# Short runs of zero matmuls in nine tile shapes at the head of TensorE's list, and other orders of the score matmuls of three chunks

## The chip, the cores and the metric

The kernel runs on one core of a Trainium2 chip. The metric is the device time of one execution in microseconds (us). The kernel before took 857.0 us, the median of two runs (855.85 and 858.14 us). The trace below is one further execution under the hardware profiler; its span is 857.2 us.

## What is computed

Two layers, each an attention block and an MLP block with residuals, over 2048 tokens of width 576, in bf16. Attention has 32 heads of 18 elements and a sliding window of 256 keys; the MLP has 4608 hidden units and tanh GELU.

```python
B, S, D, H, W, F = 1, 2048, 576, 32, 256, 4608      # Dh = 18
def A(x, wqkv, wo):                                  # attention
    q, k, v = (x @ wqkv) split in 3 and in heads
    scores = einsum("bhqd,bhkd->bhqk", q, k) * Dh ** -0.5
    mask = (i - j >= 0) & (i - j < W)
    return merge(softmax(where(mask, scores, -1e9)) @ v) @ wo
def Bm(x, w1, b1, w2, b2):                           # MLP
    return gelu(layernorm(x) @ w1 + b1) @ w2 + b2
for layer in range(2):
    x = x + A(layernorm(x), A_wqkv, A_wo)
    x = x + Bm(layernorm(x), B_w1, B_b1, B_w2, B_b2)
```

## The kernel before

The tokens are cut into chunks of 512 (four tiles of 128), four chunks for each layer, numbered k = 0 to 7 through both layers. For each chunk `qkv` makes q, k and v, `E` (`E0` for chunk 0) runs scores, exponentials, masks and the product with v for eight groups of four heads, `tail` applies `wo` and the residual, and `G_part` and `mm2` run the MLP in three parts. The stages of neighbouring chunks are interleaved.

Each engine runs its list strictly in order. The lists are made by a planner, `Plan.schedule`, from estimated costs, priorities and a table of nudges; `Sched.add` puts semaphore waits where one engine needs another's result. TensorE's work carries a mode: `f` is the full array of 128 rows and 128 columns, `r` four row tiles (32x128 each), `c` four column tiles (128x32 or 128x20), `h` two row tiles (64x128). A run of matmuls in one mode that fills all its tiles at once is called a wave below: four matmuls in `r` and `c`, two in `h`, one in `f`.

At the head TensorE has nothing to compute until the first tokens have been loaded and normalised. As soon as the tile `warm` has been set to zero (L657) it runs zero matmuls: `zero` (L662, two of 256 columns for each of the four PSUM banks 7, 6, 5 and 4), then `warm_fn` (L671, 256 columns each), whose number `keep_warm` works out from the planner's own estimates. Then come the transposes of the normalised tokens (L732), and the q, k and v matmuls of chunk 0 (L794), which wait for the loads of `wqkv`. The PSUM banks are handed out by the planner in the same way.

`scores` (L923) makes one unit of scores: for each of four heads j, which lie in the row tiles 32j to 32j+31, it multiplies the keys of one tile by the queries of one to three tiles. A unit has one or two parts n, with another key tile each. Head j has a PSUM bank of its own, and the two parts lie beside each other in it. One semaphore increment stands on the unit's last matmul; ScalarE's exponential (L933) waits for it, then GpSimd masks the diagonal blocks (L954), then the product with v follows (L975). In the chunks 1, 2 and 3 each group has three units: two with parts of 384 and 128 columns, one with 256 and 256. That is 16 and 8 units for each chunk.

Of the kernel before, what the change touches and what calls it, by code (L numbers as in the profile page):

```python
# [40 lines left out]
class Sched:  # L41
# [23 lines left out]
    def add(self, eng, fn, reads=(), writes=(), dma=None, ring=4, own=False):  # L65
        waits = {}

        def want(ev):
            c, v, _e = ev
            if waits.get(c, 0) < v:  # L70
                waits[c] = v

        for r in reads:
            lw = self.last_write.get(r)
            if lw is not None and not (eng == "pe" and lw[2] == "pe"):
                want(lw)
        for w in writes:
            for rd in self.readers.get(w, ()):
                if own or rd[2] != eng or rd[3]:
                    want(rd[:3])  # L80
            lw = self.last_write.get(w)
            if lw is not None and (own or not (eng == "pe" and lw[2] == "pe")):
                want(lw)
        if dma is None:
            assert eng != "sp"
            c = self.cnt[eng]
            amount = 1
        else:
            rg = self.ring(eng, dma, ring)
            c = rg.sems[rg.i % rg.k]  # L90
            rg.i += 1
            amount = 16
            if c.val > 0:
                want((c, c.val, None))
        wl = []
        wd = self.waited[eng]
        for cc, v in waits.items():
            if wd.get(cc, 0) >= v:
                continue
            wd[cc] = v  # L100
            wl.append((cc, v))
        c.val += amount
        by = None if dma is not None else eng
        ev = (c, c.val, by)
        self.steps[eng].append(Step(eng, fn, wl, c, amount))
        for w in writes:
            self.last_write[w] = ev
            self.readers[w] = []
        for r in reads:
            self.readers.setdefault(r, []).append((c, c.val, by, dma is not None))  # L110
        return ev
# [324 lines left out]
def build_kernel(nc, A_x, A_wqkv, A_wo, B_x, B_w1, B_b1, B_w2, B_b2, out):  # L436
# [38 lines left out]
    add = PL.add  # L475
# [66 lines left out]
    def sb(name, shape, dtype):  # L542
        return nc.alloc_sbuf_tensor(name, shape, dtype)
# [24 lines left out]
    warm = sb("warm", [P, P], BF16)  # L568
# [7 lines left out]
    def bank(i):  # L576
        if isinstance(i, Bank):
            i = i.no
        return ps[:, i * 512:(i + 1) * 512]

    FILL = (7, 6, 5, 4)
    OUT = (7, 6, 5, 4)
# [3 lines left out]
    def two(b):  # L586
        return ps[:, b.no * 512:(b.no + 2) * 512].rearrange("p (j c) -> p j c", j=2)
# [18 lines left out]
    def q_of(k):  # L606
        return (qx, "qx") if k == 1 else (qT, "q")

    def k_of(A):

        if Q1 <= A < Q1 + 2:
            return kx[:, A - Q1, :, :], f"kx{A - Q1}"
        sl = A if A < Q1 else (A - 2) % KS
        return kT[:, :, sl, :], f"k{sl}"
# [35 lines left out]
    for i in range(NQN):  # L650
        add("pool", lambda e, i=i: e.memset(qn[:, i, :].rearrange("p (h e) -> p h e", e=32)[:, :, DH:32], 0.0),
            writes=[f"qn{i}h{h}" for h in range(2)], cost=0.5, prio=-9)
    for b in range(2):
        add("dve", lambda e, b=b: e.memset(wqkv[64 * b:64 * b + 64, 4, :].rearrange("p (w s d) -> p w s d", w=3, s=2)[:, :, 1 - b, :], 0.0),
            writes=[f"w{w}C{b}" for w in "qkv"], cost=0.5, prio=-8)
# [3 lines left out]
    def zero(e, b):  # L659
        ins = None  # L660
        for c in range(2):
            ins = e.matmul(bank(b)[:, c * 256:(c + 1) * 256], warm[:, :], warm[:, :].unsqueeze(1).to_broadcast([P, 2, P]), start=True, stop=True)  # L662
        return ins
    for i in OUT:
        b = Bank((i,))
        add("pe", lambda e, b=b: zero(e, b), reads=["warm"], writes=[b], cost=0.42, lat=0.2, prio=-7, alloc=[b])

    def warm_fn(e, bk, n):
        ins = None
        for _ in range(n):  # L670
            ins = e.matmul(bank(bk)[:, 0:256], warm[:, :], warm[:, :].unsqueeze(1).to_broadcast([P, 2, P]), start=True, stop=True)  # L671
        return ins
# [238 lines left out]
    def scores(k, g, parts, prio, gs=None):  # L911
        l, t0, nt = CH[k]
        T0 = l * NT + t0
        qs, qname = q_of(k)
        sl = slots.popleft()
        bs = [Bank(SC, True), Bank(SC, True)]

        def fn(e):
            ins = None
            for n, (so, qo, nq, col) in enumerate(parts):  # L920
                gg = gs[n] if gs else g
                for j in range(4):
                    ins = e.matmul(two(bs[j // 2])[:, j % 2, col:col + nq * 128], k_of(T0 + so)[0][32 * j:32 * j + 32, gg, :],  # L923
                                   qs[32 * j:32 * j + 32, gg, qo * 128:(qo + nq) * 128], start=True, stop=True, tile_position=(32 * j, 0),
                                   skip_group_check=True)
            return ins
        rd = [f"{qname}{qo + i}" for (so, qo, nq, col) in parts for i in range(nq)] + [k_of(T0 + p[0])[1] for p in parts]
        ncol = sum(p[2] for p in parts) * 128
        add("pe", fn, reads=rd, writes=bs, cost=0.01 + ncol * 0.00042, prio=prio, lat=0.15, alloc=bs, fifo="pa", mode="r", after=[f"p{sl}h{h}" for h in range(2)] + [f"p{sl}m{m}" for m in range(3)])
        lo = min(p[3] for p in parts)  # L930
        hi = max(p[3] + p[2] * 128 for p in parts)
        for h2 in range(2):
            add("act", lambda e, h2=h2: e.activation(pT[:, sl, 2 * h2:2 * h2 + 2, lo:hi], two(bs[h2])[:, :, lo:hi],  # L933
                                                     ACT.Exp, scale=SCALE),
                reads=[bs[h2]], writes=[f"p{sl}h{h2}"], cost=0.07 + 2 * (hi - lo) * 0.00083, lat=0.17,
                fifo="act", prio=prio)
        blk = {}
        for (so, qo, nq, col) in parts:
            for q in range(nq):
                if qo + q == so:  # L940
                    blk[col + q * 128] = "d"
                elif qo + q == so + 2:
                    blk[col + q * 128] = "o"
        runs = []
        for c in sorted(blk):
            if runs and runs[-1][0] == blk[c] and runs[-1][1] + runs[-1][2] * 128 == c:
                runs[-1][2] += 1
            else:
                runs.append([blk[c], c, 1])
        for mi, (kind, col, nb) in enumerate(runs):  # L950
            sgn = 1 if kind == "d" else -1
            pat = [[0, 4]] + ([[0, nb]] if nb > 1 else []) + [[sgn, 128]]
            ap = pT[:, sl, :, col:col + nb * 128]
            add("pool", lambda e, ap=ap, pat=pat, sgn=sgn, kind=kind: e.affine_select(  # L954
                ap, ap, pattern=pat, compare_op=(ALU.is_ge if kind == "d" else ALU.is_gt), fill=0.0, base=0, channel_multiplier=-sgn),
                reads=[f"p{sl}h0", f"p{sl}h1"], writes=[f"p{sl}m{mi}"], cost=0.12 + 0.475 * nb, prio=prio)
        return sl
# [244 lines left out]
    for i in range(n0):  # L1202
# [5 lines left out]
        cost=0.5, prio=-1)  # L1208
    dma("sp", b2bc[:, :], bass.AP(tensor=B_b2.tensor, offset=B_b2.offset, ap=[[0, P], [1, D]]), reads=["k3"], writes=["b2"], cls="b", ring=2,
        cost=0.5, prio=-1)  # L1210
    add("pe", lambda e: e.transpose(bank(bb).bitcast(BF16)[:, 0:NF], b1in, ident[0:NF, 0:NF]), reads=["b1i", "ident"], writes=[bb],
        cost=0.1, lat=0.22, prio=5, alloc=[bb])
# [104 lines left out]
def bass_interleave_layers__sliding_block__mixer_channel_mlp__prompt_kernel(  # L1317
    nc,
    A_x,
    A_wqkv,  # L1320
    A_wo,
    B_x,
    B_w1,
    B_b1,
    B_w2,
    B_b2,
    out,
):
    build_kernel(nc, A_x, A_wqkv, A_wo, B_x, B_w1, B_b1, B_w2, B_b2, out)
# [28 lines left out]
```

## Time and profile before

| | |
|---|---|
| runs | 855.85 and 858.14 us, median 857.0 |
| the profiled execution | span 857.2 us |
| DVE, ACT, POOL busy | 46%, 70%, 44% |
| DMA | mean 140 GB/s |

The page gives each engine's busy time, the chain of work that ended last, and the costliest groups. The timeline gives, in order of time, the start and the length of a group of equal instructions on one engine, and in brackets how long the engine had been idle before it and what it waited for. The durations of single matmuls overlap: a matmul of 288 columns shows some 0.286 us, though the next one of the same kind starts 0.12 us later. So prices are taken from start to start, or from the length of a long group divided by its count. "x20" counts instructions, four of which make one wave in the modes `r` and `c`.

### The profile page before, as it was taken

Reading aid. Unit: us, or ns where it says so; the run is one execution under the profiler, and the core shown is the slowest. Engines: PE = TensorE matmul, PEld = TensorE weight load, DVE = VectorE, ACT = ScalarE, POOL = GpSimd, SP = SyncE. Lnnn points to the kernel's source line nnn. Section 1 sums busy time; section 2 is a strip of 40 time slices with the busy share of each in tenths; the row PEclk is TensorE's granted clock in tenths of the full one; section 3 lists DMA queues with packets and bytes.
Section 4 is the critical chain, followed back from the end, with each engine's and each line's share of the span. In section 5 each row is a group of like instructions: output and inputs, shape, how many; then the busy total and the mean of one; then the engine's idle time right before and its main releaser. Section 6 shows DMA issues by size and latency. Waiting matters only on the chain.

```text
span 857.2 us, 28212 instructions
## 1 busy us (share of the span) xinstructions
PE 842.7 (98%) x12180; PEld 517.6 (60%) x12180; DVE 398.6 (46%) x949; ACT 599.1 (70%) x745; POOL 379.1 (44%) x569
## 2 busy tenths in 40 slices
PE   8999999999999999999999999999999999999998
PEld 6555556556566565666665655656556556556556
DVE  6777434655257352672445723564226534162013
ACT  4988887778757787476773877748885689853730
POOL 4776554375235662263421654426534276322100
PEclk9999999999999999999999999999999999999999
DMA  7899435461596534967258443595345963346320
GB/s 198 195 184 149 127 124 145 115 165 45 166 182 124 154 94 121 186 133 191 85 124 195 89 149 122 104 223 130 112 157 116 225 187 109 119 133 186 116 84 29
DMA packets 181996, 119.86 MB, mean 140 GB/s; under 512 B 107504, under 2 KB 181872, under 8 KB 181872
## 3 DMA queue, kind: packets, MB, share of 16 engines
q1 hardware_dynamic: 181872, 118.05, 55.1%
q8 instruction: 96, 1.57, 0.8%
q14 instruction: 28, 0.23, 0.1%
HBM read 90.10 MB, written 2.36 MB: 108 GB/s over the span
## 4 chain that ended last, share of the span: by engine, by line
PE 91%; DMA 3%; DVE 2%; ACT 2%; POOL 1%; issue 1%; SPq 0%; DVEq 0%; POOLq 0%; ACTq 0%
PE ps L1115 31%; PE ps L775 25%; PE ps L778 11%; PE ps L835 8%; PE ps L923 6%; PE ps L975 5%; PE ps L1070 4%; DMA xnTm<-xn 2%; ACT pT L933 1%; DMA wqkv<-in_A_wqkv_dram 1%; PE ps L794 1%; DVE x_res L1047 1%; POOL pT L954 1%; DMA x_res<-qn 1%; DVE st_all L684 1%
## 5 line engine op out<-in xcount | busy, mean ns | idle before, releaser
L954 POOL TENSOR_SCALAR_AFFINE_SELECT pT<-pT 128x1024 bf16<-128x1024 bf16 (+1 forms) x370 | 282.8, 786 | 219.3 <-ACT pT L933 217.1
L933 ACT ACTIVATE pT<-ps 128x1024 bf16<-128x1024 f32 (+1 forms) x372 | 344.9, 999 | 42.4 <-PE ps L923 41.7
L1115 PE MATMUL ps<-xnTm,w_sb 64*128 64x512 bf16 x2592 | 291.8, 376 | 0.6 <-DVE x_res L1050 0.3
L1125 ACT ACTIVATE hT<-ps,b1col 128x512 bf16<-128x512 f32 x276 | 168.0, 688 | 176.5 <-PE ps L1115 176.4
L1115 PEld LDWEIGHTS ps<-xnTm,w_sb 64*128 64x128 bf16 x2592 | 127.5, 94 | 140.7 <-issue 4.0
L775 PE MATMUL ps<-w_sb,hT 128*128 128x288 bf16 x1410 | 188.5, 287 | 0.9 <-DVE vA L847 0.8
L1047 DVE TENSOR_TENSOR x_res<-ps,x_res 128x288 f32<-128x288 f32 x224 | 100.5, 454 | 180.7 <-PE ps L775 122.3
L775 PEld LDWEIGHTS ps<-w_sb,hT 128*128 128x128 bf16 x1410 | 130.5, 98 | 50.5 <-issue 16.9
L778 PE MATMUL ps<-w_sb,hT 128*32 128x288 bf16 x2808 | 96.5, 286 | 0.2
L835 PE MATMUL ps<-wqkv,xnTa 64*128 64x288 bf16 x1296 | 91.3, 283 | 2.2 <-DVE vA L847 0.9
L859 DVE CAST qn<-ps 128x288 bf16<-128x288 f32 x112 | 46.4, 451 | 86.4 <-PE ps L835 78.5
L986 DVE STREAM_TRANSPOSE oq<-ps 128x512 f32<-128x512 f32 x64 | 45.8, 716 | 84.6 <-PE ps L975 83.9
L778 PEld LDWEIGHTS ps<-w_sb,hT 128*32 128x32 bf16 x2808 | 72.5, 97 | 14.9 <-issue 3.4
L835 PEld LDWEIGHTS ps<-wqkv,xnTa 64*128 64x128 bf16 x1296 | 61.4, 94 | 30.0 <-issue 3.9
L923 PE MATMUL ps<-qT,kT 32*128 32x128 bf16 (+2 forms) x1248 | 63.2, 274 | 2.5 <-ACT pT L933 2.5
L697 POOL TENSOR_SCALAR vtmp<-mv_all 128x1 f32<-128x1 f32 (+2 forms) x45 | 9.2, 204 | 120.5 <-DVE mv_all L688 119.1
L1131 POOL TENSOR_TENSOR x_res<-x_res,b2bc 128x576 f32<-128x576 f32 x32 | 40.2, 1276 | 37.6 <-ACT hT L1125 37.4
L684 DVE BATCH_NORM_STATS2 st_all<-x_res 128x6 f32<-128x288 f32 (+1 forms) x128 | 53.5, 446 | 3.0 <-DMA x_res<-in_A_x_dram 2.1
L847 DVE CAST vA<-ps 128x288 bf16<-128x288 f32 x60 | 25.3, 448 | 55.1 <-PE ps L835 49.1
L975 PE MATMUL ps<-pT,vA 128*20 128x384 bf16 (+2 forms) x1440 | 50.4, 275 | 0.3 <-DVE vA L847 0.2
L923 PEld LDWEIGHTS ps<-qT,kT 32*128 32x128 bf16 x1248 | 19.2, 92 | 41.4 <-issue 26.9
L1070 PE MATMUL ps<-wo_sb,attT 64*128 64x288 bf16 x576 | 42.5, 283 | 0.3
(58 smaller groups left out, 478.4 us busy)
## 6 DMA issues: line engine op xcount, KB each, us to landing
w_sb<-in_B_w_dram SPq DMA_DIRECT2D x46, 864.0 KB, 6.1
w_sb<-in_B_w_dram SPq DMA_DIRECT2D x48, 768.0 KB, 4.8
w_sb<-in_B_w_dram SPq DMA_DIRECT2D x96, 48.0 KB, 4.6
wqkv<-in_A_wqkv_dram SPq DMA_DIRECT2D x3, 576.0 KB, 5.6
x_res<-in_A_x_dram SPq DMA_DIRECT2D x3, 576.0 KB, 4.3
wqkv<-in_B_w_dram SPq DMA_DIRECT2D x2, 864.0 KB, 5.2
out_dram<-x_res SPq DMA_DIRECT2D x12, 144.0 KB, 1.9
xnTm<-xn SPq DMA_TRANSPOSE x36, 2.8
```

The lines of the kernel that those rows point to most:

```text
L684: add("dve", lambda e, i=i, s=s: e.bn_stats(st_all[:, t, i, :], s[:, t, i * HB:(i + 1) * HB]), reads=res, writes=[f"st{t}_{i}"], cost=0.37 ...
L775: return e.matmul(bank(b)[:, 0:HB], lhs, rhs, start=start, stop=stop, skip_group_check=True)
L778: ins = e.matmul(bank(b)[32 * j:32 * j + 32, 0:HB], lhs[:, 32 * j:32 * j + 32], rhs, start=start, stop=stop, tile_position=(0, 32 * j), sk ...
L835: ins = e.matmul(bank(bs[o])[:, 0:HB], xnTa[r:r + 64, c, i * 128:(i + 1) * 128], wqkv[r:r + 64, c, col:col + HB], start=(c == 4), stop=(ph ...
L923: ins = e.matmul(two(bs[j // 2])[:, j % 2, col:col + nq * 128], k_of(T0 + so)[0][32 * j:32 * j + 32, gg, :], qs[32 * j:32 * j + 32, gg, qo ...
L933: add("act", lambda e, h2=h2: e.activation(pT[:, sl, 2 * h2:2 * h2 + 2, lo:hi], two(bs[h2])[:, :, lo:hi], ACT.Exp, scale=SCALE), reads=[bs ...
L954: add("pool", lambda e, ap=ap, pat=pat, sgn=sgn, kind=kind: e.affine_select(ap, ap, pattern=pat, compare_op=(ALU.is_ge if kind == "d" else ...
L975: ins = e.matmul(bank(bo)[32 * j:32 * j + VW, qo * 128:(qo + nq) * 128], vA[:, (T0 + so) % VS, 8 * j + g, :], pT[:, sl, j, col:col + nq * ...
L1047: add("dve", lambda e: e.tensor_tensor(x_res[:, t, sl], bank(b)[:, 0:HB], x_old[:, t, sl], ALU.add), reads=[b] + ([f"xin{t}"] if first els ...
L1070: ins = e.matmul(bank(bs[o])[:, 0:HB], attT[r:r + 64, c, i * 128:(i + 1) * 128], wo_sb[r:r + 64, c, col:col + HB], start=(ph == 0 and c == ...
L1115: ins = e.matmul(bank(bks[i])[:, 0:n], w1_sb[r:r + 64, sls[i], col:col + 128], xnTm[r:r + 64, k % 2, c, 0:n], start=(c == 4), stop=(ph == ...
L1125: add("act", lambda e, ff=ff, hd=hd, bk=bk: e.activation(hd[:, 0:n], bank(bk)[:, 0:n], ACT.Gelu_apprx_tanh, bias=b1col[:, ff:ff + 1]), rea ...
```

## The change

Twenty probe steps are put at the head of TensorE's list, ahead of `zero`. Each step runs a number of waves in one tile shape, on the zero tile `warm`, into the four banks that `zero` uses afterwards; nothing reads them. There are nine shapes: r (32x128), c (128x32), h (64x128), f (128x128), u (128x64), s (32x64), m (64x64), q (32x32) and t (64x32). The steps have 397 matmuls in all, each with its own load of weights, of 64 to 512 columns, and the shape changes between most of them. To the planner a step costs 0.01 us.

The score matmuls of three chunks are issued in another order; the same matmuls run. In chunk 1 the two parts alternate from head to head, and then the other halves follow. In chunk 2 the second part runs through the heads backwards. In chunk 3 the second part runs ahead of the first. All other chunks keep their order.

```diff
+    SIZES = {"r": (32, 128), "c": (128, 32), "h": (64, 128), "f": (128, 128), "u": (128, 64), "s": (32, 64), "m": (64, 64), "q": (32, 32), "t": (64, 32)}
+
+    def step(e, bks, md, n):
+        ins = None
+        rs, cs = SIZES[md]
+        for r in range(0, 128, rs):
+            for c in range(0, 128, cs):
+                rhs = warm[r:r + rs, 0:n] if n <= 128 else warm[r:r + rs, 0:n // 4].unsqueeze(1).to_broadcast([rs, 4, n // 4])
+                ins = e.matmul(bank(bks[r // rs])[c:c + cs, 0:n], warm[r:r + rs, c:c + cs], rhs, start=True, stop=True,
+                               tile_position=(r, c), skip_group_check=True)
+        return ins
+
+    PROBE = (("r", 288, 6), ("r", 64, 8), ("c", 64, 8), ("f", 64, 8), ("r", 512, 3), ("s", 288, 4), ("r", 288, 3), ("q", 288, 4), ("r", 288, 3), ("c", 288, 3),
+             ("q", 288, 3), ("t", 288, 3), ("c", 288, 3), ("u", 288, 3), ("f", 288, 3), ("u", 288, 3), ("m", 288, 3), ("h", 288, 3), ("r", 128, 6), ("h", 64, 8))
+    hs = [Bank((i,)) for i in OUT]
+    for n, (md, cols_, cnt) in enumerate(PROBE):
+        def fn(e, md=md, cols_=cols_, cnt=cnt):
+            ins = None
+            for _ in range(cnt):
+                ins = step(e, hs, md, cols_)
+            return ins
+        add("pe", fn, reads=["warm"], writes=hs, cost=0.01, lat=0.0, prio=-7.5, alloc=hs if n == 0 else ())
+
+    ORDERS = {0: lambda N: [(n, j) for n in range(N) for j in range(4)],
+              1: lambda N: [(n if j % 2 == 0 else N - 1 - n, j) for n in range(N) for j in range(4)],
+              2: lambda N: [(n, j if n == 0 else 3 - j) for n in range(N) for j in range(4)],
+              3: lambda N: [(N - 1 - n, j) for n in range(N) for j in range(4)]}
...
-            for n, (so, qo, nq, col) in enumerate(parts):
+            for n, j in ORDERS.get(k, ORDERS[0])(len(parts)):
+                so, qo, nq, col = parts[n]
                 gg = gs[n] if gs else g
-                for j in range(4):
+                if True:
                     ins = e.matmul(two(bs[j // 2])[:, j % 2, col:col + nq * 128], k_of(T0 + so)[0][32 * j:32 * j + 32, gg, :],
```

The lists of VectorE, ScalarE, GpSimd and the DMA queue are the same as before, row for row. On TensorE, the head of the list before is this (line, operation, destination and sources, shape of the destination, count):

```order
L139 UNCONDITIONAL_BRANCH
L662 MATMUL ps<-warm 128x256 x8
L671 MATMUL ps<-warm 128x256 x12
L732 MATMUL ps<-ident,xn 128x128 x5
L671 MATMUL ps<-warm 128x256 x6
L794 MATMUL ps<-wqkv,xnTa 128x288 x10
L732 MATMUL ps<-ident,xn 128x128 x4
L794 MATMUL ps<-wqkv,xnTa 128x288 x10
```

And after the change, from the last probe steps on (the lines of the file have moved by 28, so `warm_fn` is L699, the transposes are L760 and the matmuls of q, k and v L822):

```order
L676 MATMUL ps<-warm 64x288 x18
L676 MATMUL ps<-warm 128x288 x6
L676 MATMUL ps<-warm 128x128 x24
L676 MATMUL ps<-warm 128x64 x16
L662 MATMUL ps<-warm 128x256 x8
L699 MATMUL ps<-warm 128x256 x11
L760 MATMUL ps<-ident,xn 128x128 x5
L699 MATMUL ps<-warm 128x256 x6
L822 MATMUL ps<-wqkv,xnTa 128x288 x10
L760 MATMUL ps<-ident,xn 128x128 x4
L822 MATMUL ps<-wqkv,xnTa 128x288 x10
```

All the zero matmuls of before still stand behind the probe, but for one of the first twelve of `warm_fn`.

A unit of chunk 1 with parts of 384 and 128 columns, on TensorE, before (the queries of chunk 1 lie in `x_res`, its keys in `xnTm` and `kT`):

```order
L775 MATMUL ps<-wqkv,xnTm 128x288 x5
L923 MATMUL ps<-x_res,xnTm 128x384 x4
L923 MATMUL ps<-x_res,kT 128x128 x4
L835 MATMUL ps<-wqkv,xnTa 128x288 x36
```

And after:

```order
L803 MATMUL ps<-wqkv,xnTm 128x288 x5
L952 MATMUL ps<-x_res,xnTm 128x384
L952 MATMUL ps<-x_res,kT 128x128
L952 MATMUL ps<-x_res,xnTm 128x384
L952 MATMUL ps<-x_res,kT 128x128 x2
L952 MATMUL ps<-x_res,xnTm 128x384
L952 MATMUL ps<-x_res,kT 128x128
L952 MATMUL ps<-x_res,xnTm 128x384
L863 MATMUL ps<-wqkv,xnTa 128x288 x36
```

The eight matmuls stand in the same place between the same neighbours, but each group of four now has two lengths in it.

## The prediction

> **What bounds the kernel now.** I read the page first: the busy times, then the chain of work that ended last.
>
> ```profile
> span 857.2 us, 28212 instructions
> PE 842.7 (98%) x12180; PEld 517.6 (60%) x12180; DVE 398.6 (46%) x949; ACT 599.1 (70%) x745; POOL 379.1 (44%) x569
> PE 91%; DMA 3%; DVE 2%; ACT 2%; POOL 1%; issue 1%; SPq 0%; DVEq 0%; POOLq 0%; ACTq 0%
> ```
>
> TensorE has almost no idle time, and 91% of the chain is its own work. So what is added to its list costs its length, unless it falls where TensorE waits. The change adds at the head, so I read the timeline there (TensorE's rows and one of ScalarE's), and under it three pieces of the chain in the same stretch.
>
> ```profile
> 1.04 1.89 PE L662 MATMUL ps<-warm 128*128 128x256 bf16 x8 [1.04 <-DVE warm L657]
> 2.72 2.69 PE L671 MATMUL ps<-warm 128*128 128x256 bf16 x12
> 5.62 0.50 PE L732 MATMUL ps<-ident,xn 128*128 128x128 bf16 x5 [0.21 <-DVE xn L715]
> 5.96 0.82 PE L671 MATMUL ps<-warm 128*128 128x256 bf16 x6
> ...
> 6.16 0.69 ACT L735 COPY xnTa<-ps 128x640 bf16<-128x640 bf16 x1 [0.32 <-PE ps L732]
> ...
> 7.62 1.39 PE L794 MATMUL ps<-wqkv,xnTa 128*128 128x288 bf16 x10 [0.84 <-DMA wqkv<-in_A_wqkv_dram]
> 8.84 0.39 PE L732 MATMUL ps<-ident,xn 128*128 128x128 bf16 x4
> 10.03 1.39 PE L794 MATMUL ps<-wqkv,xnTa 128*128 128x288 bf16 x10 [0.81 <-DMA wqkv<-in_A_wqkv_dram]
> 11.25 0.50 PE L732 MATMUL ps<-ident,xn 128*128 128x128 bf16 x6
> 12.01 1.39 PE L794 MATMUL ps<-wqkv,xnTa 128*128 128x288 bf16 x10 [0.25 <-DMA wqkv<-in_A_wqkv_dram]
> ```
> ```profile
> 2.19 4.94 DMA wqkv<-in_A_wqkv_dram
> 7.14 4.62 DMA wqkv<-in_A_wqkv_dram
> 12.01 1.02 PE ps L794 x7
> ```
>
> Up to 12.01 us the three loads of `wqkv` set the pace; TensorE fills the time with zero matmuls and waits for each load. That is the only cover the probe has. From there the chain goes on over TensorE, and ScalarE's and VectorE's work follows TensorE's, so a later start is passed on to the end.
>
> **Prices.** Tiled modes are priced by waves, from start to start.
>
> ```profile
> 49.48 1.40 PE L775 MATMUL ps<-wqkv,xnTm 128*128 128x288 bf16 x10
> 50.81 0.34 PE L923 MATMUL ps<-qT,kT 32*128 32x384 bf16 x4
> 51.08 0.67 PE L975 MATMUL ps<-pT,vA 128*20 128x384 bf16 x16
> 51.58 0.79 PE L778 MATMUL ps<-wqkv,xnTm 128*32 128x288 bf16 x20
> 52.29 0.34 PE L923 MATMUL ps<-qT,kT 32*128 32x256 bf16 x8
> ```
> ```profile
> 101.13 2.94 PE ps L778 x96
> 87.54 11.76 PE ps L1115 x108
> ```
> ```profile
> 369.76 0.40 PE L923 MATMUL ps<-qT,kT 32*128 32x128 bf16 x16
> ```
> ```profile
> L923 PE MATMUL ps<-x_res,xnTm 32*128 32x384 bf16 x64 | 5.5, 331 | 0.4 <-ACT pT L933 0.4
> L923 PE MATMUL ps<-x_res,kT 32*128 32x128 bf16 x64 | 3.6, 214 | 0.0
> L923 PE MATMUL ps<-x_res,kT 32*128 32x256 bf16 x64 | 3.2, 273 | 0.1
> ```
>
> - A wave of 288 columns: 96 column-tile matmuls are 24 waves in 2.94 us, 0.1225 us each.
> - A wave of 512: 108 row-tile matmuls are 54 waves in 11.76 us, 0.218 us each. By columns from the first price, 128 columns take 0.054 us, 256 take 0.109 and 384 take 0.163.
> - A change of shape: ten full matmuls from 49.48 take 1.225 us, yet the next shape begins at 50.81, 0.105 late; the wave of 384 from 50.81 to 51.08 is 0.107 over its 0.163; five waves from 51.58 to 52.29 are 0.10 over 0.61. So 0.10 us each.
> - The clock: the first eight zero matmuls start 1.68 us apart in all (1.04 to 2.72), 0.21 each, where 256 columns should take 0.109. The engine runs at half speed at first; by 5.96 six take 0.82 with the last one's overlap, full speed. The end of the slow stretch lies between 5.07 (where the last slow one starts) and 5.62; I take 5.2.
> - Small tiles: the sixteen 32x128 matmuls of 128 columns at 369.76 take 0.40 us; without the last one's 0.214 that leaves 0.186 for 15 steps, 0.0124 us a matmul. That is the densest group of the trace.
>
> **The probe.** Of the 47 waves of 288 columns 40 are not in shape q: 40 x 0.1225 = 4.90 us. A q wave has sixteen matmuls: by columns 0.1225 us (lower end), by the densest group 16 x 0.0124 = 0.20. The upper end is the steady rate of the column tiles, 0.1225/4 = 0.0306 us a matmul, which gives 0.49. I take 0.20, since that row is nearest in shape and kept up its pace: 7 x 0.20 = 1.40. Three waves of 512 are 0.65, six of 128 are 0.33. For the 32 waves of 64 columns (r, c, f and h, eight each) columns alone give 0.027 us, and the wave of the densest group 4 x 0.0124 = 0.05, which I take since no shorter wave is shown: 1.60. Nineteen changes of shape, the last one into the zero matmuls, at 0.10: 1.90. About twelve of them are between shapes that the trace has not got; they could cost nothing, or up to 0.15. Sum at full clock: 4.90 + 1.40 + 0.65 + 0.33 + 1.60 + 1.90 = 10.78 us. The slow stretch, 1.04 to 5.2, does in 4.2 us what full speed does in 2.1, so 2.1 more: the probe lasts 12.9 us.
>
> It begins at 1.04 and ends at 13.94. Behind it stand 8 + 11 zero matmuls, now at full speed: 19 x 0.109 = 2.07. The first transposes begin at 16.0 instead of 5.62, 10.4 late. Of this the waits for loads give back: the q matmuls stand 2.00 behind the transposes (5.62 to 7.62); with the load there they wait only for ScalarE's copy, which ends at 6.16 + 0.69 = 6.85, 1.23 behind them, so about 1.25. The k matmuls stand 2.41 behind q, and need 1.22 + 0.22 = 1.44; the v matmuls 1.98 behind k, and need 1.22 + 0.34 = 1.56. That is 0.75 + 0.97 + 0.42 = 2.1 us. The loads are DMAs that wait for nothing on TensorE, so they have all landed by 12. What is late next is the transposes' copies and casts, which follow TensorE. Net 10.4 - 2.1 = +8.3 us. The missing zero matmul is in this count.
>
> **The score orders.** They run beside nothing: TensorE is busy for 78.90 of the 81 us in which chunk 1's scores lie.
>
> ```profile
> 60.00:141.00 81.00, 78.90 (x1200) 46.15 (x1198) 38.64 (x91) 70.20 (x92) 46.46 (x69) 1.00 0.56 128
> 60.15 0.34 PE L923 MATMUL ps<-x_res,xnTm 32*128 32x384 bf16 x4
> 60.31 0.24 PE L923 MATMUL ps<-x_res,kT 32*128 32x128 bf16 x4
> ```
>
> Now the second wave starts 0.16 us after the first, one length of 384. In chunk 1 the order is 384, 128, 384, 128 and then 128, 384, 128, 384 on the row tiles 0 to 3. If starts keep the order of the list, the fifth matmul waits for tile 0 (384 columns), and tile 1, free after 128, stands idle behind it: 384 + 384 columns instead of 384 + 128, so 256 columns or 0.109 us more. There are sixteen such units (the 64 matmuls of 384 above, in fours); the eight of 256 and 256 lose nothing. +1.74 us; if each row tile takes its next matmul by itself, zero. I take 1.74, since the one increment on a unit's last matmul already counts on that order. The Trainium skill (TensorE: Matmul & The Clock Gate, section The mechanism) says that matmuls start and end strictly in program order, reordering nothing but weight loads. By that the term is 1.74; no wave of two lengths is in the trace, so zero stays as the other end. In chunk 2 the second part begins with the tile that started last in the first; four starts spread over 0.34 - 0.331 = 0.009 us, so about 0.01 for each of 24 units, +0.24. In chunk 3 the short wave goes first and the columns stay the same: 0, at most the same 0.24. Exponentials and masks wait for the unit's end either way. Sum +2.0.
>
> **The sum.** +8.3 + 2.0 = +10.3 us on the profiled 857.2, 867.5. The median of the runs is 0.2 lower: 867.3 us, 1.2% slower, which is within the 2% that a measurement of this kernel can tell from no change.
>
> **Rivals.** First, TensorE's sequencer cannot feed the small tiles.
>
> ```profile
> 434.72 1.16 PE L975 MATMUL ps<-pT,vA 128*20 128x384 bf16 x40
> 435.70 0.54 PE L778 MATMUL ps<-w_sb,hT 128*32 128x288 bf16 x12
> ```
>
> These 40 matmuls take 0.98 us, 0.0245 each; no longer group is denser. If a matmul costs that much whatever its shape: q waves 0.39 (+1.35), s and t waves 0.20 (+0.5), 64-column waves in four tiles 0.10 (+0.8), the 128s +0.25, sum +2.9 and less where the clock is slow anyway: 870 us; at 0.0306 us a matmul 871. For it: 397 matmuls have never stood so close. Against it: the sixteen at 369.76 went twice as fast. The Trainium skill (TensorE: Matmul & The Clock Gate, section Wait — 56ns, not 53.3ns?) gives about 25 ns as a floor from start to start, which speaks for this rival; the starts of the sixteen contradict it as a rule for every matmul.
>
> Second, slower than 2%: instructions do not arrive in time.
>
> ```profile
> q8 instruction: 96, 1.57, 0.8%
> q14 instruction: 28, 0.23, 0.1%
> w_sb<-in_B_w_dram SPq DMA_DIRECT2D x96, 48.0 KB, 4.6
> ```
>
> Ninety-six fetches bring 1.57 MB, 16 KB each, one in 8.9 us over the span. With the 0.23 MB of the other instruction queue, 28212 instructions are 64 bytes each. The probe's 397 matmuls and 397 weight loads are 51 KB, three fetches in 13 us at the head. If TensorE stood still for each as long as a 48 KB load takes to land, 4.6 us, that is 13.8 more: 881 us. It decides from 6.8 us on (867.3 to 874.1), 2.3 a fetch. Against it: in the 40 dense matmuls there is no gap, so fetches run ahead.
>
> Third, cheaper: the twelve unseen changes are free (-1.2), q waves cost columns alone (-0.5), waves of 64 columns too (-0.7), the orders cost nothing (-2.0). With all of it 863. The clock can add or take as much:
>
> ```profile
> 53.00:56.40 3.40, 1.80 (x20) 0.70 (x22) 1.96 (x5) 3.40 (x6) 3.05 (x5) 1.00 1.23 142
> 56.40:59.80 3.40, 3.40 (x48) 1.79 (x49) 2.09 (x5) 1.22 (x2) 1.91 (x4) 0.50 0.97 270
> ```
>
> After a stretch in which TensorE was busy for 1.80 of 3.4 us the clock was at half for 3.4 us, which costs 1.7 us. In the changed kernel this may fall away, or come twice, and the first slow stretch may last one such window longer.
>
> **How the numbers follow.** My sum, 865 to 870: 0.50. The feeding rival, 870 to 872.5: 0.22. Cheaper, 862 to 865: 0.18. Fetches, above 874: 0.07. The rest 0.03, below 862 or between. The range 862.5 to 872.5 leaves out the fetches, the rest and the edges of the others, under 2 in 10. Slower by over 2% (above 874.1) is the fetch rival and a little of the feeding one, 0.08; faster by over 2% needs a loss of the whole probe and more, 0.01; the rest, 0.91, is within 2%.
>
> **What would show it.** In the profile after, the transposes begin near 16 us and the waits of L794 (now L822) for `wqkv` are gone; the q waves start 0.20 us apart; changes of shape cost 0.10; a mixed unit of chunk 1 is 0.11 us longer than before; the rest of the trace is shifted by some 10 us and otherwise equal. Transposes before 13 or after 19 us would mean that the price of small tiles or of changes is wrong; a later shift that grows outside the chunks 1 to 3 would mean that the lists wait for each other in a way that I have not seen.

## The result, and the profile after

The changed kernel took 867.35 us (median of two runs, 867.08 and 867.62) against 857.0 us: 1.0116 times the time before, 95% interval 1.0078 to 1.0154. That is slower by about 10 us, and less than the 2% named in the prediction. Each run's time is 1.7 us longer than its span (867.08 and 865.4 us for the profiled one), so the spans of the two profiles differ by less, 8.2 us: the profiled execution before was some 2 us slower than its kernel's usual run.

The page of the changed kernel, first its span and busy times, then the instruction queue and the chain of work that ended last:

```profile
span 865.4 us, 29004 instructions
PE 850.8 (98%) x12576; PEld 522.6 (60%) x12576; DVE 398.7 (46%) x949; ACT 598.8 (69%) x745; POOL 379.0 (44%) x569
...
q8 instruction: 99, 1.62, 0.8%
...
PE 90%; DMA 3%; DVE 3%; ACT 2%; issue 1%; POOL 1%; DVEq 0%; POOLq 0%; ACTq 0%; SPq 0%
```

TensorE has 396 matmul records more and 8.1 us more busy time, the other engines are as busy as before, and three more blocks of instructions were fetched (99 instead of 96). The timeline of TensorE at the head:

```profile
1.04 6.54 PE L676 MATMUL ps<-warm 32*128 32x288 bf16 x223 [1.04 <-DVE warm L657]
8.76 5.72 PE L676 MATMUL ps<-warm 32*128 32x288 bf16 x174 [1.18 <-issue]
14.41 1.05 PE L662 MATMUL ps<-warm 128*128 128x256 bf16 x8
15.30 1.36 PE L699 MATMUL ps<-warm 128*128 128x256 bf16 x11
16.50 0.44 PE L760 MATMUL ps<-ident,xn 128*128 128x128 bf16 x5
16.78 0.82 PE L699 MATMUL ps<-warm 128*128 128x256 bf16 x6
17.77 1.39 PE L822 MATMUL ps<-wqkv,xnTa 128*128 128x288 bf16 x10 [0.17 <-issue]
18.99 0.39 PE L760 MATMUL ps<-ident,xn 128*128 128x128 bf16 x4
19.21 1.39 PE L822 MATMUL ps<-wqkv,xnTa 128*128 128x288 bf16 x10
20.44 0.50 PE L760 MATMUL ps<-ident,xn 128*128 128x128 bf16 x6
20.77 1.46 PE L822 MATMUL ps<-wqkv,xnTa 128*128 128x288 bf16 x10
```

The probe lasts from 1.04 to 14.41, with 1.18 us in it in which TensorE shows no matmul and waits for nothing that the profile knows ("issue"). The waits for `wqkv` in front of L822 are gone. Where the rest of the time went is read by setting the start of the same matmul in both timelines side by side:

| matmul | before, us | after, us | later by |
|---|---|---|---|
| first transposes | 5.62 | 16.50 | 10.88 |
| first v matmul of chunk 0 | 12.01 | 20.77 | 8.76 |
| `qkv` of chunk 1 (L778/L806) | 56.36 | 64.07 | 7.71 |
| first `qkv` of chunk 2 behind the first unit of chunk 1 (L835/L863) | 60.85 | 67.03 | 6.18 |
| an `mm2` matmul | 100.19 | 107.13 | 6.94 |
| an MLP matmul | 360.31 | 367.25 | 6.94 |
| `qkv` (L835/L863) | 470.26 | 478.08 | 7.82 |
| near the end | 835.50 | 843.61 | 8.11 |

So the head costs 8.8 us. The loss of 2.6 up to 67 us is not the change's: in the execution before, TensorE waited 1.06 us for a late transpose at 56.36 us and then ran at half clock for 3.4 us, and the profile after shows neither. Nor does the profile of `e1_orders` below, which has no probe. From 100 to 360 us, in which chunks 2 and 3 run with their new score orders, nothing is added. The later steps are waits for other late transposes: behind the scores of chunk 3 the shift grows by 1.2 us, which the prediction named as a sign of waits that it had not seen. TensorE's waits in the changed kernel (total us, times, longest):

```profile
PE ps L863 <- DVE vA L875: 1.2, 1, 1.2
PE ps L676 <- issue: 1.2, 1, 1.2
...
PE ps L863 <- DMA xnTa<-xn: 1.0, 1, 1.0
PE ps L803 <- DVE x_res L1076: 0.7, 1, 0.7
PE ps L952 <- DMA kT<-qn: 0.7, 1, 0.7
```

And the clock of the changed kernel in that stretch, in the view by windows (busy time of TensorE, its weight loads, VectorE, ScalarE and GpSimd, then the granted clock):

```profile
56.00:59.00 3.00, 3.00 (x44) 1.81 (x37) 2.50 (x6) 2.75 (x4) 2.25 (x4) 1.00 1.15 215
59.00:63.00 4.00, 3.81 (x66) 2.14 (x65) 3.46 (x8) 3.91 (x7) 3.30 (x6) 1.00 0.78 150
```

From start to start in the trace, the waves of the probe took (us; the first wave of a step stands apart, since it takes longer behind a change of shape). Half clock is read here from the pace, twice the time for the same columns; the trace's first record of the clock, full clock, is at 4.95 us, and the views print 1.00 for the time before it as well.

| step | each wave | first wave of a step | change to the next shape, over the wave |
|---|---|---|---|
| r, c, f of 64 columns, half clock | 0.053 | 0.045 to 0.070 | 0.12 to 0.13 |
| h of 64 columns, full clock | 0.029 | 0.039 | 0.10 |
| r, c, t, f, h of 288 | 0.122 | 0.132 to 0.134 | 0.09 to 0.115 |
| s, u, m of 288 | 0.122 | 0.147 | 0.10 to 0.115 |
| q of 288, mean of the step without its change | 0.173 and 0.186 | 0.134 | 0.10 |
| r of 128 | 0.056 | 0.066 | 0.10 |

The means of q are those of short steps. In the step of four q waves the starts lie 0.134, 0.185 and 0.133 us apart, and the sixteen starts of the last wave are spread over 0.125 us, which the change behind it waits for. What a longer run of q waves costs was not tried.

### The profile page after: what moved, and what is told of

It reads as the page before. It is cut to its first block, busy times and chain, and to the rows that moved or that the text cites. A ratio compares the mean times of both kernels' runs of the same rounds, so it can differ in the third digit from the quotient of the medians.

```text
span 865.4 us, 29004 instructions
## 1 busy us (share of the span) xinstructions
PE 850.8 (98%) x12576; PEld 522.6 (60%) x12576; DVE 398.7 (46%) x949; ACT 598.8 (69%) x745; POOL 379.0 (44%) x569
## 4 chain that ended last, share of the span: by engine, by line
PE 90%; DMA 3%; DVE 3%; ACT 2%; issue 1%; POOL 1%; DVEq 0%; POOLq 0%; ACTq 0%; SPq 0%
PE ps L1144 30%; PE ps L803 24%; PE ps L806 10%; PE ps L863 8%; PE ps L952 6%; PE ps L1004 5%; PE ps L1099 3%; ACT pT L962 2%; DMA xnTm<-xn 2%; PE ps L676 1%; PE ps L822 1%; DVE x_res L1076 1%; DMA xnTa<-xn 1%; DVE st_all L712 1%; DMA kT<-qn 1%
## 5 line engine op out<-in xcount | busy, mean ns | idle before, releaser
L806 PE MATMUL ps<-w_sb,hT 128*32 128x288 bf16 x2808 | 96.5, 286 | 0.2
L863 PE MATMUL ps<-wqkv,xnTa 64*128 64x288 bf16 x1296 | 91.5, 283 | 3.1 <-DVE vA L875 1.2
L806 PEld LDWEIGHTS ps<-w_sb,hT 128*32 128x32 bf16 x2808 | 72.5, 97 | 14.9 <-issue 3.6
L863 PEld LDWEIGHTS ps<-wqkv,xnTa 64*128 64x128 bf16 x1296 | 61.1, 94 | 31.4 <-issue 3.6
```

Of the source, the lines that this page charges most:

```text
L806: ins = e.matmul(bank(b)[32 * j:32 * j + 32, 0:HB], lhs[:, 32 * j:32 * j + 32], rhs, start=start, stop=stop, tile_position=(0, 32 * j), sk ...
L863: ins = e.matmul(bank(bs[o])[:, 0:HB], xnTa[r:r + 64, c, i * 128:(i + 1) * 128], wqkv[r:r + 64, c, col:col + HB], start=(c == 4), stop=(ph ...
```

## The experiments

Theory A is the prediction's mechanism with the score orders at zero: only the time that TensorE needs at the head counts, less what the loads of `wqkv` hide, and each row tile takes its next matmul by itself. Theory B is the prediction's own price of the orders: matmuls start in the order of the list. The rivals C to I are named where they come in. "Before" is measured again in each set, on the same chip.

**The two halves alone.** `e1_orders` is the changed kernel without the probe:

```diff
-    PROBE = (("r", 288, 6), ("r", 64, 8),
...
-        add("pe", fn, reads=["warm"], writes=hs, cost=0.01, lat=0.0, prio=-7.5, alloc=hs if n == 0 else ())
```

> The score orders of the chunks 1, 2 and 3 alone, no probe. Theory A (each row tile takes its next matmul by itself, so that a short matmul in one tile does not hold back the others): the time of the kernel before, 857 us, within 1 us. Theory B (matmuls start in the order of the list): 2.0 us more, 859 us; a unit of chunk 1 with parts of 384 and 128 columns takes 0.11 us longer to its successor on TensorE.

Measured: 856.5 us against 856.78 for the kernel before, ratio 0.9996 (0.9987 to 1.0005).

`e2_probe` is the changed kernel with the orders of before:

```diff
-            for n, j in ORDERS.get(k, ORDERS[0])(len(parts)):
-                so, qo, nq, col = parts[n]
+            for n, (so, qo, nq, col) in enumerate(parts):
                 gg = gs[n] if gs else g
-                if True:
+                for j in range(4):
```

> The probe alone, score orders as before. Theory A: all of the change's time is the probe's, so the same as the changed kernel, 867.3 us within 1 us, with the first transposes at 16.5 us. Theory B: 2 us less than the changed kernel, 865.3 us.

Measured: 868.18 us, ratio 1.0129 (1.0111 to 1.0146). The orders cost nothing, the probe everything; B falls.

**The orders, sharper.** `e3_bytile` runs the score matmuls of all chunks tile by tile, which a strict order of starts would punish most:

```diff
-            for n, (so, qo, nq, col) in enumerate(parts):
+            for n, j in [(n, j) for j in range(4) for n in range(len(parts))]:
+                so, qo, nq, col = parts[n]
```

> The kernel before with the score matmuls of all chunks issued tile by tile (both parts of head 0, then both of head 1, and so on), no probe. Theory A: each tile works down its own two matmuls, no change, 857 us within 1 us, or a little more if the weight loads of the later tiles come late. Theory B: the first matmul of each tile waits behind the second one of the tile ahead of it; a unit of 384 and 128 columns takes 0.48 us more and one of 256 and 256 takes 0.33 more, about 10 us for each of six chunks: 915 us or more.

Measured: 858.72 us, ratio 1.0021 (1.0012 to 1.0030): 1.9 us where B asked for 58 or more. How it works is read in the changed kernel's own trace, in the timeline of the first mixed unit of chunk 1 (order in the list: 384, 128, 384, 128 on the tiles 0 to 3, then 128, 384, 128, 384):

```profile
66.70 0.32 PE L952 MATMUL ps<-x_res,xnTm 32*128 32x384 bf16 x1 [0.35 <-ACT pT L962]
66.70 0.22 PE L952 MATMUL ps<-x_res,kT 32*128 32x128 bf16 x1
66.71 0.33 PE L952 MATMUL ps<-x_res,xnTm 32*128 32x384 bf16 x1
66.71 0.22 PE L952 MATMUL ps<-x_res,kT 32*128 32x128 bf16 x1
66.77 0.33 PE L952 MATMUL ps<-x_res,xnTm 32*128 32x384 bf16 x2
66.86 0.23 PE L952 MATMUL ps<-x_res,kT 32*128 32x128 bf16 x2
67.03 1.15 PE L863 MATMUL ps<-wqkv,xnTa 64*128 64x288 bf16 x16
```

The two 384s of the second half start at 66.77, when their tiles have finished 128 columns, and the two 128s that stand ahead of them or between them in the list start at 66.86, when theirs have finished 384. So a tile does not wait for another tile's turn, and the list's order is not the order of the starts: that each engine runs its list strictly in order, as said above, does not hold for TensorE's row tiles. The unit's one increment stands on the last matmul of the list, a 384. Here that one is also the last to end, by 0.003 us in the trace, whose ends are modelled; no run shows an order in which another tile would end clearly later. From 66.70 to the next work at 67.03 the unit takes 0.33 us, as the plain order does: over all units of two parts behind 60 us the median from the first start to the successor's is 0.329 us before, after and in `e1_orders`. In `e3_bytile` it is 0.339, and 0.01 us for each of these 160 units is 1.6 of the 1.9 us. What costs the 0.01 was not tried.

**Shapes or length?** `e4_plain` puts 93 matmuls of one shape in the probe's place:

```diff
-    PROBE = (("r", 288, 6), ("r", 64, 8),
...
+    PROBE = (("f", 288, 93),)
```

> The probe replaced by 93 zero matmuls of the full array, 288 columns each, all of one shape, to last about as long as the probe did (13.4 us: some 17 waves at half clock and 76 at full clock); score orders as before. Theory A (only the length at the head counts): 867.3 us within 1 us, transposes at 16.5 us, and no idle stretch inside the filler, since its 186 instructions come slowly. Rival (the tile shapes or their changes leave something behind, or the stretch of 1.18 us without work inside the probe comes from the loads of the inputs and not from the instructions): another time by over 1.5 us, or the idle stretch at 7.6 to 8.8 us is there as well.

Measured: 866.06 us, ratio 1.0104 (1.0089 to 1.0118). The timeline of its head:

```profile
1.04 13.73 PE L676 MATMUL ps<-warm 128*128 128x288 bf16 x93 [1.04 <-DVE warm L657]
14.60 1.04 PE L662 MATMUL ps<-warm 128*128 128x256 bf16 x8
```

No idle stretch, and the head is as long as the probe's. The first transposes begin at 16.79 us, 0.3 later than in the changed kernel. But the time is 2.1 us under the probe's and 1.3 under the changed kernel's, so A holds for the head and misses something behind it; see the last two sets.

**What is the idle stretch?** Three answers: C, instructions come in blocks of 256 and too late; D, the input loads; E, the way back from 32x32 tiles. `e5_double` runs the probe twice:

```diff
-    for n, (md, cols_, cnt) in enumerate(PROBE):
+    for n, (md, cols_, cnt) in enumerate(PROBE + PROBE):
```

> The probe twice, one pass behind the other, score orders as before. The second pass runs at full clock and needs 10.1 us by the waves of the first. Theory C (the idle stretch of 1.2 to 1.4 us in the probe is TensorE waiting for its instructions, which come in blocks of 256, that is 128 matmuls with their loads): idle stretches stand every 128 matmuls, behind some 224, 352, 480, 608 and 736 of them, wherever the list is used up faster than the blocks come, whatever the shape there; the second pass takes 11.5 to 14 us, the kernel 880 to 882 us. Theory D (the stretch comes from the loads of the inputs, which fill the DMA engines up to 12 us): no idle stretch behind 12 us, 878.3 us. Theory E (it comes with the change from 32x32 back to four row tiles): one behind each of these changes, at the matmuls 216 to 224 of each pass.

Measured: 878.99 us, ratio 1.0255 (1.0239 to 1.0271), between D's 878.3 and C's 880. The place of the idle stretches decides; the timeline of its head:

```profile
1.04 6.93 PE L676 MATMUL ps<-warm 32*128 32x288 bf16 x223 [1.04 <-DVE warm L657]
9.86 7.13 PE L676 MATMUL ps<-warm 32*128 32x288 bf16 x256 [1.89 <-issue]
17.88 3.18 PE L676 MATMUL ps<-warm 128*32 128x64 bf16 x128 [0.89 <-issue]
21.61 6.10 PE L676 MATMUL ps<-warm 32*32 32x288 bf16 x187 [0.55 <-issue]
```

The idle stretches stand behind 223, 479 and 607 matmuls: multiples of 128 apart, one of them in the middle of the c steps and one inside a 32x32 step, two of them long behind the input loads (the DMA queues move 0.02 MB from 13.0 to 15.2 us). The single probe shows the same grid, in the timeline of `e2_probe`, behind 223 and 351:

```profile
1.04 6.09 PE L676 MATMUL ps<-warm 32*128 32x288 bf16 x223 [1.04 <-DVE warm L657]
8.49 4.46 PE L676 MATMUL ps<-warm 32*128 32x288 bf16 x128 [1.36 <-issue]
13.33 1.33 PE L676 MATMUL ps<-warm 64*128 64x288 bf16 x46 [0.38 <-issue]
```

128 matmuls with their 128 loads are one block of 256 instructions (16 KB of 64 bytes). E falls, and so does D as the cause of the later stretches. The traces hold the packets of the instruction queue as well (q8 in the views), 16 KB each, and so show C at work. This is the view of the DMA queues in `e5_double` from 15.2 to 16.7 us, with one packet and no other:

```profile
DMA packets 1, 0.02 MB, mean 11 GB/s; under 512 B 0, under 2 KB 0, under 8 KB 0
...
q8 instruction: 1, 0.02, 5.5%
```

It lands at 16.62 us, and TensorE goes on at 17.88. Each idle stretch ends in this way, 1.25 to 1.53 us behind a landing:

| run | packet landed, us | TensorE goes on, us | later by |
|---|---|---|---|
| changed kernel | 7.43 | 8.76 | 1.33 |
| `e2_probe` | 6.99 and 11.79 | 8.49 and 13.33 | 1.50 and 1.53 |
| `e5_double` | 8.34, 16.62 and 20.36 | 9.86, 17.88 and 21.61 | 1.52, 1.26 and 1.25 |

`e8_noq` replaces the 32x32 steps by fewer, larger matmuls of the same time:

```diff
-    PROBE = (("r", 288, 6), ("r", 64, 8), ("c", 64, 8), ("f", 64, 8), ("r", 512, 3), ("s", 288, 4), ("r", 288, 3), ("q", 288, 4), ("r", 288, 3), ("c", 288, 3),
-             ("q", 288, 3), ("t", 288, 3), ("c", 288, 3), ("u", 288, 3), ("f", 288, 3), ("u", 288, 3), ("m", 288, 3), ("h", 288, 3), ("r", 128, 6), ("h", 64, 8))
+    PROBE = (("r", 288, 6), ("r", 64, 8), ("c", 64, 8), ("f", 64, 8), ("r", 512, 3), ("s", 288, 4), ("r", 288, 3), ("f", 288, 6), ("r", 288, 3), ("c", 288, 3),
+             ("f", 288, 5), ("t", 288, 3), ("c", 288, 3), ("u", 288, 3), ("f", 288, 3), ("u", 288, 3), ("m", 288, 3), ("h", 288, 3), ("r", 128, 6), ("h", 64, 8))
```

> The probe with the two steps of 32x32 tiles (64 and 48 matmuls) replaced by 6 and 5 waves of the full array, of the same time but with 101 matmuls less. Theory C (instruction blocks): the list is used up more slowly, the idle stretch behind matmul 224 falls at about 10 us, when the block has come, and vanishes; 1.4 to 1.8 us less than the probe alone, 866.5 us. Theory D (input loads): TensorE stands still at 7 to 9 us as before, 868.2 us. Theory E (32x32) also says that it vanishes; it is told apart by the doubled probe.

Measured: 865.77 us, ratio 1.0104 (1.0090 to 1.0118), 2.4 us under the probe alone, more than C's 1.4 to 1.8. Its head, in the timeline, has no idle stretch, and the zero matmuls follow at 12.97 instead of 14.59:

```profile
1.04 11.99 PE L676 MATMUL ps<-warm 32*128 32x288 bf16 x296 [1.04 <-DVE warm L657]
12.97 1.05 PE L662 MATMUL ps<-warm 128*128 128x256 bf16 x8
```

The packet lands at 7.08 us here, and TensorE needs its block only at 9.76. C stands. In `e5_double`, where TensorE runs into the limit again and again, two blocks pass between the resumptions at 9.86 and 17.88 and one between 17.88 and 21.61: 3.7 to 4.0 us a block, so at most one matmul with its load in 29 to 31 ns over a longer stretch. Early on a block can take longer: 4.8 us pass between the two resumptions of `e2_probe`, 5.4 (8.50 to 13.88) in `e10_probe`. Whether the input loads have a part in that was not tried.

**The cover, and the filler behind.** `e6_short` keeps the first five steps of the probe:

```diff
-    PROBE = (("r", 288, 6), ("r", 64, 8),
...
+    PROBE = (("r", 288, 6), ("r", 64, 8), ("c", 64, 8), ("f", 64, 8), ("r", 512, 3))
```

> Only the first five steps of the probe (r 288, r 64, c 64, f 64, r 512: 4.1 to 4.2 us, 108 matmuls), score orders as before. Theory A with the cover as predicted (the head hides 4.6 us of added work, since the loads of wqkv set the pace up to 12 us): no change, 856.8 us within 0.8 us, though the first transposes begin at 7.3 us, 1.7 later than before. Rival F (a later start of the first transposes is passed on to the end): 858.5 us.

Measured: 857.51 us against 856.93, ratio 1.0013 (1.0003 to 1.0022): between the two, nearer to A. The timeline of its head:

```profile
7.61 0.44 PE L754 MATMUL ps<-ident,xn 128*128 128x128 bf16 x5
...
12.68 1.39 PE L816 MATMUL ps<-wqkv,xnTa 128*128 128x288 bf16 x10 [0.16 <-issue]
```

The first transposes are 2.0 us later than before, the v matmuls only 0.7. A part comes back at 21.81 us, where the first scores waited 1.2 us for a late transpose of q, which the kernel before does not show. `e7_nofill` has the whole probe, but not the 19 zero matmuls behind it:

```diff
-    for i in OUT:
-        b = Bank((i,))
-        add("pe", lambda e, b=b: zero(e, b), reads=["warm"], writes=[b], cost=0.42, lat=0.2, prio=-7, alloc=[b])
...
-    PL.warm_from = 0.6
+    PL.warm_from = 5.4
```

> The probe alone, with the 19 zero matmuls behind it taken out (zero and the first run of the filler). Theory A: the filler stands on the path behind the probe, so 2.1 us less than the probe alone, 866.1 us. Rival G (behind the probe something else sets the pace, so that the filler is hidden): the same as the probe alone, 868.2 us.

Measured: 864.89 us, ratio 1.0095 (1.0079 to 1.0110). The v matmuls of chunk 0 start at 18.97 instead of 20.95, 2.0 us sooner, as A says; by the medians the gain over the probe alone is 3.3, over the changed kernel 2.5. The filler is on the path; G falls.

**The 2 us behind the head.** The same three kernels again on one chip:

> The changed kernel again, beside the next two on one chip, to measure the three against each other. Theory A: 867.4 us within 1 us.

> The probe alone again. Theory A: the same as the changed kernel within 0.7 us, since the score orders cost nothing; the 868.2 us of the first four runs were high by late transposes in some of them.

> The 93 full-array zero matmuls again, whose head was as long as the probe's (the v matmuls of chunk 0 at 21.06 and 20.95 us). Theory A: the same as the probe alone within 0.7 us. Rival: 2 us less, as in the first runs; then something behind the head, in the stretches at 73, 380, 478 and 584 us where TensorE waited for late transposes in the probe's profile, differs for good.

Measured: 867.06, 867.93 and 865.28 us, ratios 1.0141 (1.0119 to 1.0163), 1.0130 (1.0116 to 1.0144) and 1.0102 (1.0088 to 1.0116). The changed kernel and the probe alone differ by 0.9 us, a little more than A's 0.7, with intervals that overlap; the plain filler is 1.8 to 2.7 us under them again, so its rival holds. TensorE's waits in the plain filler (`e11_plain`), and then in the probe alone (`e2_probe`):

```profile
PE ps L945 <- DMA qT<-qn: 0.9, 1, 0.9
PE ps L857 <- ACT qn L878: 0.6, 1, 0.6
PE ps L1137 <- DVE x_res L1072: 0.3, 1, 0.3
PE ps L997 <- DVE vA L869: 0.2, 1, 0.2
PE ps L797 <- DVE qn L881: 0.2, 1, 0.2
```
```profile
PE ps L858 <- DMA xnTa<-xn: 2.4, 2, 1.3
PE ps L676 <- issue: 1.7, 2, 1.4
PE ps L798 <- DVE x_res L1070: 1.4, 1, 1.4
PE ps L858 <- DVE vA L870: 1.1, 1, 1.1
```

The probe's waits for `xnTa`, `x_res` and `vA`, 1.0 us and more each at some 73, 380, 480 and 585 us, are missing or small in the plain filler. `e12_tiny` asks whether they hang on where the instruction blocks end. It has the plain filler's list, instruction for instruction, with 64 columns:

```diff
-    PROBE = (("f", 288, 93),)
+    PROBE = (("f", 64, 93),)
```

> The same 93 full-array zero matmuls as the plain filler, but of 64 columns: 93 times 0.053 us at half clock, at most 4.9 us, close to what the head hides. TensorE's list is instruction for instruction as long as the plain filler's, so its instruction blocks end at the same matmuls. Theory H (the 2 us by which the plain filler stays under the probe at an equal head hang on where the blocks of 256 instructions end): the waits at some 470 and 575 us that the kernel before has become small, and the time is 1 to 2 us under the kernel before, 855 us. Rival I (they hang on the time at which TensorE runs against the transfers): the time of the short probe, 0 to 0.7 us over the kernel before, with the waits at 470 or 575 us as there.

Measured: 857.66 us against 857.48, ratio 1.0003 (0.9992 to 1.0014). In its one profile the waits at 470 and 575 us are gone, as H says, but the time is I's, the kernel before's: the first scores waited 1.5 us for q at 21.96 us, the filler having pushed the first transposes to 7.22 us. In all three profiles with this list these waits are 0.4 us or less, and the kernel before and every probe of 397 matmuls has one or two of 0.8 us and more at 470 to 585 us. How a list's length acts on transposes 450 us later was not shown; it stays open, and so does the question whether such a list without the late q would beat the kernel before.

## Why the prediction was right

The mechanism held in the main: the time is what TensorE spends at the head, less what the loads of `wqkv` had hidden. 867.35 us were measured for 867.3 forecast, which is nearer than the steps deserve: two errors cancel, and that is luck.

- The probe: 12.9 us forecast, 13.37 measured (1.04 to 14.41). Its waves took 12.0 and the late instructions 1.35 more than a wave. The q waves, at a mean of 0.173 to 0.186 us, lay near the 0.20 that the densest group gave, though their starts lie 0.13 to 0.19 apart and not 0.20 as forecast; the nineteen changes lay at 0.10 as read from the kernel's own changes (0.12 to 0.13 at half clock), the unseen ones among them. The waves of 64 columns follow their columns (0.053 us at half clock, 0.029 at full), less than the 0.05 at full clock in the sum. The longer first wave, 0.011 to 0.025 us, was left out.
- What the head gives back: 2.1 us forecast, 10.88 - 8.76 = 2.1 measured.
- The score orders: this step failed. 2.0 us were put down, 1.74 of them because starts should keep the order of the list; `e1_orders` measured -0.3 us with an interval from -1.1 to +0.4, and the median unit of two parts stayed at 0.329 us. The Trainium skill (TensorE: Matmul & The Clock Gate, section The mechanism), which was weighed there, says that matmuls start strictly in program order. The trace here disagrees for row tiles: of eight matmuls the sixth in the list starts at 66.77 us, ahead of the fifth at 66.86. Zero was the other end of that term.
- In place of the 2.0 us stand about 0.5 more at the head and 1 to 2 us of waits behind it that were not in the sum. They differ from list to list and from run to run, and `e4_plain` and `e11_plain` show that a head of the same length can go without most of them.
- The first rival, feeding, was right in kind at another price: not a price for every small matmul, since the q steps take 11 to 12 ns a matmul, but a stop where the next block has not landed. The second, late fetches, named the cause and mis-sized it, 1.2 us once instead of 4.6 three times. The dense 40 matmuls that spoke against it are shorter than a block, so they could not show it.
- The clock: the half-clock stretch at 56 us fell away in the profiled run, as the third rival allowed; its 1.7 us is part of why the spans differ by 8.2 and the medians by 10.35.
- The sum set the span of one execution equal to the runs' time. The time is 1.7 us longer, and the execution before was that much slower than its median; in the forecast the two cancel.

## What to carry to other kernels

Work added at the head costs its length less the wait that it covers, and the cover is read from the transfers that set the pace there; even inside the cover a later first step may come back as a late transfer. Row tiles work down their own matmuls, so two lengths on four tiles need no careful order, as long as each tile has the same sum (tiles of unlike sums were not tried). A dense stretch of small matmuls is free only as far as its instructions have landed, which was 223 matmuls into the list here; beyond that 256 instructions took 3.7 to 5.4 us to come, however short they are.

## What was not expected of the hardware

- Matmuls on different row tiles start out of the order of the list, up to 0.1 us (66.77 ahead of 66.86).
- TensorE stops at the ends of instruction blocks: behind 223, 351, 479 or 607 matmuls of the list, for 0.4 to 1.9 us, until 1.25 to 1.53 us after the 16 KB packet with the next block has landed.
- The first wave behind a change of shape takes 0.011 us longer for tiles of 32 or 128 columns and 0.025 for tiles of 64 columns, and the change itself 0.10 us at full clock whichever the two shapes are.
- In steps of three and four waves, sixteen 32x32 tiles cost 0.17 to 0.19 us a wave of 288 columns, against 0.122 for four tiles.
